# A shifted copy of V sent in three parts, and new order lists for all five engines

## The chip, the core and the metric

The kernel runs on one core of one Trainium2 chip. That core has five instruction streams that matter here: TensorE (PE, matrix multiplication, with PEld for its weight loads), VectorE (DVE), ScalarE (ACT), GpSimd (POOL) and SyncE (SP), which in this kernel only issues DMAs. SBUF is the on-chip memory of 128 partitions, and PSUM is the memory of eight banks that PE writes into. The metric is the device time in microseconds (us) of one execution. Most executions of one kernel agree within 0.3%.

## The reference

The kernel computes a fused mixer on 2048 tokens of width 512, in bf16: a sliding, dilated local attention, a gated MLP that mixes over tokens, and the residual.

```python
def _A_ref(x, wqkv, wo):                     # 32 heads of 16, window 8, dilation 2
    qkv = (x @ wqkv).reshape(B, S, 3, H, Dh).transpose(2, 0, 3, 1, 4)
    q, k, v = qkv[0], qkv[1], qkv[2]
    idx = pos[:, None] - off[None, :]        # off = 0, 2, ..., 14
    mask = idx >= 0
    ...
    logits = jnp.einsum('bhsd,bhswd->bhsw', q, kg) * scale
    logits = jnp.where(mask[None, None, :, :], logits, -1000000000.0)
    attn = _softmax(logits, axis=-1)
    o = jnp.einsum('bhsw,bhswd->bhsd', attn, vg)
    return o.transpose(0, 2, 1, 3).reshape(B, S, D) @ wo

def _B_ref(x, w_in, w_sp, b_sp, w_out):      # Fh = 896
    z = _gelu(jnp.einsum('bsd,df->bsf', x, w_in))
    z1 = z[..., :Fh].copy()
    z2 = _layernorm(z[..., Fh:], axis=-1)
    g = jnp.einsum('ts,bsf->btf', w_sp, z2) + b_sp[None, :, None]
    return jnp.einsum('bsf,fd->bsd', z1 * g, w_out)

x = A_x
xn = _layernorm(x, axis=-1)
return x + _A_ref(xn, A_wqkv, A_wo) + _B_ref(xn, B_w_in, B_w_sp, B_b_sp, B_w_out)
```

## The kernel before, in words

**Layout.** The 2048 tokens are cut into 16 blocks of 128. In the working layout a token is 16 times its partition plus its block number q, so that one block holds every sixteenth token. The keys of a token lie 0, 2, ..., 14 tokens back. A token of block q therefore needs the values V of blocks q, q-2, ... on its own partition, and where q-2i is negative, it needs block q-2i+16 of the partition before it. For these the kernel keeps a shifted copy: 14 columns of tokens in front of V, in which partition p+1 holds what partition p holds in blocks 2 to 15. It is made by two DMAs from SBUF to SBUF, Vhaloa for partitions 0 to 111 and Vhalob for 112 to 126 (L1155), and by Vzero (L1158), which puts zeros on partition 0. The products of the probabilities with V (pv0 to pv15, L1178, one DVE instruction for each block) read both V and the copy; pv14 and pv15 need no copy, since they reach back 14 tokens at most.

**Order.** The program is a list of about 760 tasks. `Plan` (L15 to L285) derives the waits from what each task reads and writes (keys with address ranges; ranges that overlap depend on each other), and gives each engine a queue of its own with one semaphore. The order in each queue isn't found by a planner here: `plan.orders` (from L1277) holds five written lists, for PE, ACT, DVE, POOL and SP, and names every task of the engine in turn. An engine works strictly down its list. A task that isn't ready holds up all that stand behind it.

**Stages on PE**, with names as the lists have them (block or group number behind the name):

- Start: the first block is centred on DVE and ACT (ctr), transposed on PE (xTr, L691), evacuated from PSUM by ACT (xTe, L698), and multiplied into z2 for blocks 0 to 3 in half pieces (z2_b_h, L900). xNr (L711) transposes the normalized first block (norm0, L675). Blocks 4 to 15 are transposed by DMA on SP's queue (xTd, L679).
- Q and K (L743, evacuated by ACT, QKe at L751) in four groups of blocks, with the rest of z2 (L877, evacuated as z2g) between them. z2s (L932) are ACT's squares of z2 for the layer norm; zm0, zq, zv, zr, zb are its small sums, of which zr (L949) runs on POOL and zb (L951) on DVE. hm (L583) are masks made on POOL.
- Logits: DVE multiplies Q with shifted K (prod, L766) and adds pairs (padd, L774); PE sums them (lg, L801); ACT evacuates them (lge, L810). Then z1 (L920, z1g) and V (L727, evacuated by ACT as Ve, L731).
- Softmax on DVE (sm, ssub, sz, L826 to L867), whose probabilities are transposed in by DMA (pT, L819).
- The token mixing: for each of eight groups t, PE does seven products P1 to P7 of 8 matmuls each (L1038), with the spatial weights w (loaded transposed by DMA, w1_0 and so on, L985), and their sums S13, S2, S4, made on DVE (L997 to L1003). The gating follows (g11, g21 on ACT, L1056; g12, g22 on DVE, L1080 and L1084; u, L1062; uT, a DMA transposition, L1064).
- pv, pva, pvc on DVE (L1178 to L1186) make the attention's output, OTd (L1190) transposes it by DMA, and out (L1240, L1244) multiplies both halves by their output weights. os and fin copy the result out of PSUM with the residual, and st (L1215) stores it.

SP's queue holds, in this order around the copy of V: pT3, pT2, pT0, pT1, w1_0, w1_1, Vhalob, Vhaloa, w2_0, w2_1, uT14. The dependency of the copy is all of V from block 2 on, and by its ranges, which name one element in each of two buffers for the logits' products, all the work on these too.

Of the kernel before, what the change touches and what calls it, by code (L numbers as in the profile page):

```python
# [14 lines left out]
class Plan:  # L15
# [301 lines left out]
    warm=28,  # L317
    fill0=1,
# [9 lines left out]
def build_kernel(nc, A_x, A_wqkv, A_wo, B_x, B_w_in, B_w_sp, B_b_sp, B_w_out, out, report=False, sched_kw=None,  # L328
# [5 lines left out]
    NB = S // 128  # L334
# [17 lines left out]
    off = {}  # L352
# [66 lines left out]
    with ExitStack() as es:  # L419
        ar = es.enter_context(nc.sbuf_tensor("arena", [128, ARENA_E], BF))  # L420
# [27 lines left out]
        R = plan.reg  # L448
# [38 lines left out]
        for i, nm in enumerate("abz"):  # L487
            R("Vh" + nm, "sb", [(off["pb"] + 4096 * s_ + 1024 + i, off["pb"] + 4096 * s_ + 1025 + i) for s_ in range(2)])
# [61 lines left out]
        def dma(eng, fn, nbytes, chan, reads=(), writes=(), name="", xbar=False, prio=None, lat=1700.0):  # L550
# [12 lines left out]
          name="steps0")  # L563
# [590 lines left out]
        for nm, p0, p1 in (("a", 0, 112), ("b", 112, 127)):  # L1154
            dma("sp", (lambda p0, p1: lambda e: e.dma_start(  # L1155
                ar[p0 + 1: p1 + 1, off["V"] - 14 * 512: off["V"]], ar[p0: p1, off["V"] + 1024: off["V"] + 8192]))(p0, p1),
                (p1 - p0) * 14 * 1024, "Vh" + nm, reads=[("V", q) for q in range(2, NB)], writes=["Vh" + nm], name="Vhalo" + nm)
# [102 lines left out]
        for t in range(NT):  # L1260
# [11 lines left out]
            if t >= 1:  # L1272
# [6 lines left out]
                warm xTr0b fill0 xTr0a z2_0_0b z2_0_1b z2_0_0a xTr1a xTr1b z2_0_1a xNr z2_1_0a z2_1_0b z2_1_1a xTr2a  # L1279
                xTr2b z2_1_1b z2_2_0a z2_2_0b xTr3b xTr3a z2_2_1a z2_2_1b z2_3_0a z2_3_1a z2_3_1b z2_3_0b Q0_0 Q0_2  # L1280
                Q0_1 K0_1 Q0_3 K0_0 K0_2 K0_3 Q1_0 K1_0 K1_1 Q1_1 Q1_2 K1_2 K1_3 Q1_3 z2_4 z2_5 z2_6 z2_7 K2_0 K2_1
                Q2_1 Q2_0 K2_2 Q2_2 z2_8 Q2_3 K2_3 z2_9 z2_10 z2_11 K3_0 Q3_1 K3_1 K3_2 Q3_2 Q3_0 z2_12 z2_13 K3_3
                Q3_3 lg0_0 z1_14 z2_15 z2_14 z1_13 z1_12 z1_15 z1_11 z1_8 z1_10 z1_6 z1_9 z1_7 z1_5 z1_4 z1_2 z1_0
# [12 lines left out]
                lge1 zn6 z1g12 z1g13 z1g15 z2s13 z1g11 z2s14 z1g8 z1g10 zn4 halo2_0 halo2_1 z1g6 z2s15 z1g9 z1g7 zn7
                z1g5 zn11 z1g4 z1g2 zn8 z1g0 zn0 z1g3 zn3 Ve12 Ve13 z1g1 Ve15 Ve14 lge2 ldxr0 lge3 Ve9 Ve10 zn9 Ve7
                Ve11 Ve6 ldxr1 Ve8 zn10 Ve4 Ve5 sexp3 Ve2 cA_0 Ve1 Ve3 Ve0 cE_0 cB_0 g11_0 os12_0 os15_0 sexp2 cA_1
                cE_1 g21_0 cB_1 g11_1 cA_2 sexp1 g11_2 os14_0 cB_2 cE_2 fin15_0 g21_1 g21_2 cA_3 cB_3 ldxr2 fin14_0
                g11_3 cE_3 os13_0 fin12_0 sexp0 cA_4 st0_0_0 g21_3 cB_4 fin13_0 g11_4 os11_0 os10_0 cE_4 ldxr3 cA_5  # L1300
                fin11_0 os8_0 ldxr4 st1_0_0 cB_5 fin10_0 cE_5 os9_0 g11_5 g21_4 os6_0 ldxr5 cA_6 cE_6 g21_5 cB_6 g11_6
                st2_0_0 fin8_0 os7_0 fin9_0 ldxr6 fin6_0 cA_7 os4_0 fin7_0 os2_0 os5_0 st3_0_0 cB_7 ldxr7 cE_7 g21_6
                g11_7 st4_0_0 fin5_0 os0_0 fin4_0 st5_0_0 g21_7 os3_0 fin2_0 fin3_0 os1_0 st6_0_0 os1_1 fin0_0 os1_2
# [15 lines left out]
                g22_5 pvc4 g12_5 u7 S2_6 pv4 pv5 u5 u4 pva2048_5 S4_6 pva1024_5 S13_7 sattn0 pvc5 g22_6 pv3 g12_6 pv2
# [65 lines left out]
```

## Time and profile before

| | us |
|---|---|
| runs | 226.03, 226.43, 226.57 (median 226.43) |
| the profiled execution | 226.05 |
| its span | 224.3 |
| PE busy | 220.5 (98%) |
| DVE busy | 207.6 (93%) |
| ACT busy | 134.2 (60%) |
| POOL busy | 92.8 (41%) |
| DMA engines, mean share by q1 and q10 | 56.6% and 6.6% |

The span runs from the first to the last instruction of the core; the execution's own time lies 1.75 us above it. In the rows of the profile a number behind L is the line of the kernel. "A <- B" means that A waited for B, "xN" is the number of instructions in a group, and an engine name with q behind it (SPq) is that engine's DMA queue. The chain of waits lists, in order of time, the pieces of work that set the end, each with its start, its length and its line. In the table by stage each engine has its busy time in the window and, in brackets, its instructions. "Us to landing" is the time from a DMA's issue to the arrival of its data.

### The profile page before, as it was taken

The page shows a single profiled execution, that of the slowest core. Times are in us where ns is not written, and L with a number is a line of the kernel's source. Part 1 is how long each engine was busy: PE and PEld are TensorE (multiplying, and loading weights), DVE is VectorE, ACT ScalarE, POOL GpSimd, SP SyncE. Part 2 cuts the span into 40 slices and gives each one's busy share as a digit, 9 for nine tenths or more (in the row PEclk, how much of TensorE's full clock was granted, in tenths as well). Part 3 has the DMA queues.
Part 4 walks back from the last instruction along what each step waited for, and adds up shares of the span by engine and source line. Part 5 has one row for each costly group of instructions (what it writes and reads, how often), then busy time and mean ns, then how long its engine had stood idle before and what let it go on. Part 6 is the DMA issues. An engine that isn't in the chain of part 4 may idle for free.

```text
span 224.3 us, 3127 instructions
## 1 busy us (share of the span) xinstructions
PE 220.5 (98%) x1176; PEld 121.4 (54%) x1176; DVE 207.6 (93%) x236; ACT 134.2 (60%) x241; POOL 92.8 (41%) x38
## 2 busy tenths in 40 slices
PE   7999999999999999999999999999999999999995
PEld 6555555554577775665555544445545544455444
DVE  4699999899999999999999999999999999999910
ACT  4758989989999999987332321525115433242442
POOL 4348289826054071000000399992899920000000
PEclk9999999999999999999999999999999999999999
DMA  6886443491000005759899896495996792729442
GB/s 218 261 200 155 63 115 69 78 274 26 3 0 0 0 0 167 172 122 220 223 154 197 215 223 120 122 217 107 139 213 167 156 173 71 163 85 168 102 92 94
DMA packets 77400, 29.96 MB, mean 134 GB/s; under 512 B 68669, under 2 KB 75339, under 8 KB 77259
## 3 DMA queue, kind: packets, MB, share of 16 engines
q1 hardware_dynamic: 74250, 25.08, 56.6%
q10 hardware_dynamic: 3136, 4.69, 6.6%
q8 instruction: 9, 0.15, 0.3%
q14 instruction: 5, 0.04, 0.0%
HBM read 9.05 MB, written 2.10 MB: 50 GB/s over the span
## 4 chain that ended last, share of the span: by engine, by line
PE 90%; DVE 4%; issue 2%; ACT 2%; DMA 1%; ACTq 0%
PE ps L1038 38%; PE ps L920 11%; PE ps L1244 11%; PE ps L743 9%; PE ps L727 6%; PE ps L1240 6%; PE ps L877 5%; DVE arena L774 3%; PE ps L900 3%; DMA arena<-in_A_x_dram 1%; PE ps L801 1%; ACT arena L751 0%; PE ps L691 0%; ACT arena L932 0%; ACT arena L883 0%
## 5 line engine op out<-in xcount | busy, mean ns | idle before, releaser
L1038 PE MATMUL ps<-arena 128*128 128x448 f16 (+1 forms) x448 | 86.6, 352 | 0.0
L860 POOL TENSOR_TENSOR arena<-arena,fpool 128x128 bf16<-128x128 f32 x2 | 48.5, 24274 | 47.1 <-DVE arena L856 47.1
L1038 PEld LDWEIGHTS ps<-arena 128*128 128x128 f16 (+1 forms) x448 | 43.7, 98 | 41.4 <-issue 0.2
L1178 DVE TENSOR_TENSOR arena<-arena 128x4096 bf16<-128x4096 bf16 x16 | 36.1, 2282 | 0.0
L766 DVE TENSOR_TENSOR arena<-arena 128x8192 bf16<-128x8192 bf16 (+1 forms) x10 | 35.5, 3558 | 0.0
L949 POOL TENSOR_TENSOR fpool<-fpool 128x4 f32<-128x4 f32 x4 | 21.0, 5255 | 25.4 <-DVE fpool L946 25.4
L743 PE MATMUL ps<-arena 128*128 128x512 bf16 x128 | 28.5, 379 | 0.0
L1182 DVE TENSOR_TENSOR arena<-arena 128x4096 bf16<-128x4096 bf16 (+1 forms) x16 | 28.0, 1749 | 0.0
L1253 ACT ACTIVATE arena<-ps 128x512 bf16<-128x512 f32 (+2 forms) x17 | 9.6, 563 | 30.6 <-PE ps L1244 30.6
L1244 PE MATMUL ps<-arena 128*128 128x512 bf16 (+2 forms) x126 | 27.1, 355 | 0.0
L774 DVE TENSOR_TENSOR arena<-arena 128x4096 bf16<-128x4096 bf16 (+1 forms) x9 | 27.0, 2995 | 0.0
L665 POOL TENSOR_TENSOR fpool<-fpool 128x1 f32<-128x1 f32 x16 | 18.8, 1183 | 14.5 <-DVE fpool L663 14.5
L1053 ACT ACTIVATE ps<-ps 128x448 f32<-128x448 f32 x16 | 8.5, 528 | 27.2 <-PE ps L1038 19.2
L920 PE MATMUL ps<-arena 128*128 128x448 bf16 x128 | 24.6, 353 | 0.0
L920 PEld LDWEIGHTS ps<-arena 128*128 128x128 bf16 x128 | 18.4, 144 | 6.1 <-issue 0.4
L743 PEld LDWEIGHTS ps<-arena 128*128 128x128 bf16 x128 | 14.4, 113 | 13.1 <-issue 0.4
L877 PE MATMUL ps<-arena 128*128 128x448 bf16 x96 | 19.0, 353 | 0.0
L1244 PEld LDWEIGHTS ps<-arena 128*128 128x128 bf16 x126 | 11.9, 98 | 12.4
L751 ACT ACTIVATE arena<-ps 128x1024 bf16<-128x1024 f32 x16 | 16.0, 1028 | 4.2 <-PE ps L743 3.5
L1240 PE MATMUL ps<-arena 128*128 128x512 bf16 (+2 forms) x72 | 16.8, 355 | 0.0
L932 ACT ACTIVATE arena<-arena 128x896 bf16<-128x896 bf16 x16 | 15.4, 965 | 0.0
L1056 ACT ACTIVATE arena<-ps,fpool 128x448 bf16<-128x448 f32 x16 | 10.0, 633 | 7.9 <-PE ps L1038 7.9
(86 smaller groups left out, 255.8 us busy)
## 6 DMA issues: line engine op xcount, KB each, us to landing
arena<-in_A_x_dram ACTq DMA_DIRECT2D x8, 256.0 KB, 2.8
arena<-in_A_x_dram SPq DMA_DIRECT2D x15, 128.0 KB, 2.3
out_dram<-arena ACTq DMA_DIRECT2D x7, 256.0 KB, 2.1
arena<-arena SPq DMA_DIRECT2D x1, 1568.0 KB, 11.1
arena<-in_A_wqkv_dram SPq DMA_DIRECT2D x3, 512.0 KB, 4.0
arena<-in_B_w_in_dram SPq DMA_DIRECT2D x1, 896.0 KB, 5.4
arena<-in_B_w_out_dram SPq DMA_DIRECT2D x1, 896.0 KB, 5.0
arena<-arena SPq DMA_TRANSPOSE x40, 3.2
```

The lines of the kernel that those rows point to most:

```text
L743: last = t.matmul(bank(k + which), AC(off["wqk"] + 1024 * dc + col0, [[4, 128]]), AC(off["xnT"] + dc * S + 512 * j, [[1, 512]]), start=(dc ...
L766: T("dve", lambda v: v.tensor_tensor(pbv, qb, kb, ALU.mult), reads=[(t_, c, j) for t_ in ("QT", "KT", "KTpad") for c in cs], writes=[("pb" ...
L774: T("dve", lambda v: v.tensor_tensor(av, av, bv, ALU.add), reads=[("pb", s_) for s_ in b], writes=[("pb", s_) for s_ in a], est=c_dve(4096 ...
L860: T("pool", lambda g: g.tensor_tensor(Rv, Zv, FCa(foff["mone"], [[0, 128]]), ALU.pow), reads=[kz, "mone"], writes=[kr], est=20000, name="s ...
L877: last = t.matmul(ps[:, 512 * (k + hf): 512 * (k + hf) + HF], AC(off["xnT"] + dc * S + 128 * b, [[1, 128]]), AC(off["w_in2"] + FH * dc + H ...
L920: lastm = t.matmul(ps[:, 512 * (k + hf): 512 * (k + hf) + HF], AC(off["xnT"] + dc * S + b, [[NTOK, 128]]), AC(off["w_in1"] + FH * dc + HF ...
L949: T("pool", lambda g: g.tensor_tensor(Fv("rstd2", 4, 4 * j), Fv("msq", 4, 4 * j), mhalf, ALU.pow), reads=[("msq", j), "mhalf"], writes=[(" ...
L1038: last = t_.matmul(pb_(k_), st(k), mv(k), start=(start and k == 0), stop=(k == 7), skip_group_check=True)
L1178: T("dve", (lambda iv, tv, av: lambda v: v.tensor_tensor(tv, iv, av, ALU.mult))(iv, tv, av), reads=[("attn", q // 4)] + [("V", i_) for i_ ...
L1182: T("dve", (lambda n: lambda v: v.tensor_tensor(AC(off["Vs"], [[4096, 2], [1, n]]), AC(off["Vs"], [[4096, 2], [1, n]]), AC(off["Vs"] + n, ...
L1240: t_.matmul(po, AC(off["OT"] + 1024 * (t % 3) + 512 * r_ + 128 * cc, [[1, 128]]), AC(off["wo"] + 512 * cc + c0, [[1, n]]), start=False, st ...
L1244: last = t_.matmul(po, AC(off["z1"] + FH * tb + 128 * fc, [[1, 128]]), AC(off["w_out"] + 512 * fc + c0, [[1, n]]), start=False, stop=(fc = ...
```

## The change

The shifted copy gets three groups of token columns instead of one: the four columns just before V (blocks 12 to 15), the four before them (blocks 8 to 11) and the last six (blocks 2 to 7). Each group is sent in the same two parts by partitions as before, so there are six DMAs (Vhalo0a to Vhalo2b) instead of two. Each waits only for its own blocks of V. Its address range names one element at its own destination. A product pv needs only the groups that it reaches into: pv10 to pv13 group 0, pv6 to pv9 groups 0 and 1, pv0 to pv5 all three.

All five order lists are written anew. Besides the six DMAs they hold the same tasks. No instruction of PE, ACT, DVE or POOL is added, removed or resized. In the kernel after, lines from the copy on stand 4 to 13 further down.

```diff
-        for i, nm in enumerate("abz"):
-            R("Vh" + nm, "sb", [(off["pb"] + 4096 * s_ + 1024 + i, ...) for s_ in range(2)])
+        VH = ((1, 4), (5, 8), (9, 14))
+        vh = lambda g_, i: off["V"] - 512 * VH[g_][1] + i
+        for g_ in range(3):
+            for i in range(2):
+                R(("Vh", g_, i), "sb", [(vh(g_, i), vh(g_, i) + 1)])
+        R("Vhz", "sb", [(vh(g_, 2), vh(g_, 2) + 1) for g_ in range(3)])
...
-        for nm, p0, p1 in (("a", 0, 112), ("b", 112, 127)):
-            dma("sp", (lambda p0, p1: lambda e: e.dma_start(
-                ar[p0 + 1: p1 + 1, off["V"] - 14 * 512: off["V"]], ar[p0: p1, off["V"] + 1024: off["V"] + 8192]))(p0, p1),
-                (p1 - p0) * 14 * 1024, "Vh" + nm, reads=[("V", q) for q in range(2, NB)], writes=["Vh" + nm], name="Vhalo" + nm)
+        def v_halo(g_):
+            lo, hi = VH[g_]
+            o_, n = off["V"] - 512 * hi, 512 * (hi - lo + 1)
+            for i, (p0, p1) in enumerate(((0, 112), (112, 127))):
+                dma("sp", (lambda p0, p1: lambda e: e.dma_start(ar[p0 + 1: p1 + 1, o_: o_ + n], ar[p0: p1, o_ + 8192: o_ + 8192 + n]))(p0, p1),
+                    (p1 - p0) * 2 * n, ("Vh", g_, i), reads=[("V", q) for q in range(16 - hi, 17 - lo)], writes=[("Vh", g_, i)],
+                    name="Vhalo%d%s" % (g_, "ab"[i]))
+        for g_ in range(3):
+            v_halo(g_)
...
-                  reads=[...] + (["Vha", "Vhb", "Vhz"] if q < 14 else []),
+                  reads=[...] + (["Vhz"] if q < 14 else []) + [("Vh", g_, i_) for g_ in range(3) for i_ in range(2) if q < 15 - VH[g_][0]],
...
 plan.orders, PE:
-  warm xTr0b fill0 xTr0a z2_0_0b z2_0_1b z2_0_0a xTr1a xTr1b z2_0_1a xNr z2_1_0a z2_1_0b z2_1_1a xTr2a
+  warm xTr0b fill0 xTr0a xNr z2_0_0b z2_0_1b xTr1a z2_0_1a xTr1b z2_0_0a z2_1_0a z2_1_1a xTr2a z2_1_0b
...
-  P1_1 P4_0 P5_1 bits P6_1 P2_1 P7_1 P3_1 P1_2 P4_1 P2_2 P5_2 P6_2 P1_3 P7_2 P3_2 out15_0 P4_2 out14_0
+  P1_1 P4_0 P5_1 P6_1 P2_1 P7_1 P3_1 P1_2 P4_1 P5_2 P6_2 P2_2 P7_2 P3_2 P1_3 P4_2 P5_3 P2_3 P6_3 out15_0
...
 ACT:
-  zn2 QKe3_1 z2s10 QKe3_2 QKe3_0 zn1 z2g12 z2g13 halo2_3 z2s11 QKe3_3 lge0 zn5 z1g14 z2s12 z2g15 z2g14
+  QKe3_2 halo2_0 halo2_3 zn3 QKe3_0 z2g12 zn1 z2g13 QKe3_3 lge0 halo2_2 z2s10 z1g14 z2s11 z2g15 z2g14
...
 DVE:
-  prod1_2 zq1 zb0 prod1_0 zv1 padd1_0 padd1_1 zb1 zq2 prod2_0 prod2_2 zv2 padd2_0 prod3_2 zq3 padd2_1
+  prod1_0 zb0 prod1_2 zq1 padd1_0 zq2 padd1_1 zv1 prod2_0 prod2_2 zq3 zb1 padd2_0 zv2 prod3_2 zv3
...
-  srec3 sm2_2 sattn3 sm3_2 pv15 pv14 g22_0 ssub2 S13_1 g12_0 sz1_2 S2_1 u14 sz2_2 pva2048_0 S4_1
+  sm1_2 srec3 sm2_2 sattn3 sm3_2 pv15 pv14 g22_0 ssub2 g12_0 S13_1 sz1_2 S2_1 sz2_2 pva2048_0 sm1_1 u15
...
 POOL:
-  rstd5 rstd10 rstd11 rstd9 mask1 rstd8 rstd14 rstd13 rstd12 rstd15 hm2 zr0 zr1 zr2 zr3 srec1 srec0
+  rstd5 rstd10 rstd8 rstd9 mask1 rstd11 rstd14 rstd15 rstd13 rstd12 zr0 hm2 zr1 zr2 zr3 srec1 srec0
...
 SP:
-  ldx0 ldx1 ldw_in2a_0 ldw_in2b_0 ldx3 ldx6 ldx7 ldx4 ldq ldx5 ldx9 ldx10 ldk ldx11 xTd6 xTd7 xTd4 xTd5
+  ldx0 ldx1 ldw_in2a_0 ldw_in2b_0 ldx3 ldx7 ldx6 ldx4 ldq ldx5 ldx10 ldk ldx9 ldx8 xTd7 xTd6 xTd4 xTd5
...
-  ldwout Vzero pT3 pT2 pT0 pT1 w1_0 w1_1 Vhalob Vhaloa w2_0 w2_1 uT14 w3_0 uT15 OTd0 ldwo0 ldwo3 ldwo2
-  ldwo1 w3_1 w4_0 uT12 OTd1 uT13 w4_1 w5_0 uT11 uT10 OTd2 w5_1 w6_0 uT8 w6_1 uT6 uT9 w7_0 OTd3 uT7 w7_1
+  ldwout pT3 pT2 Vhalo0a Vhalo1b pT0 w1_0 w1_1 pT1 w2_0 ldwo3 ldwo2 Vzero w2_1 ldwo0 Vhalo2b ldwo1
+  Vhalo0b uT14 w3_0 uT15 w3_1 uT12 OTd0 w4_0 uT13 w4_1 Vhalo1a uT11 OTd1 w5_0 uT10 w5_1 OTd2 Vhalo2a uT8
```

More of the change, by code (lines that the diff above doesn't have):

```diff
@@ L1278, in build_kernel @@
             """
-                warm xTr0b fill0 xTr0a z2_0_0b z2_0_1b z2_0_0a xTr1a xTr1b z2_0_1a xNr z2_1_0a z2_1_0b z2_1_1a xTr2a
[L1280 to L1283, printed above, removed]
@@ new lines, in build_kernel @@
+                xTr2b z2_1_1b z2_2_1a xTr3a xTr3b z2_2_0a z2_2_1b z2_2_0b z2_3_1a z2_3_0a z2_3_1b z2_3_0b Q0_0 Q0_2
+                Q0_1 K0_1 Q0_3 K0_0 K0_2 K0_3 K1_0 Q1_0 Q1_1 K1_1 K1_2 Q1_2 Q1_3 K1_3 z2_4 z2_5 z2_6 z2_7 Q2_0 K2_0
+                K2_1 Q2_1 Q2_2 Q2_3 K2_3 z2_8 K2_2 z2_10 z2_11 z2_9 K3_1 Q3_1 K3_2 Q3_2 Q3_0 K3_0 z2_12 z2_13 Q3_3
+                K3_3 lg0_0 z1_14 z2_15 z2_14 z1_13 z1_12 z1_15 z1_8 z1_11 z1_10 z1_7 z1_6 z1_9 z1_2 z1_5 z1_4 z1_1
+                z1_0 z1_3 V13 V12 V10 V14 lg2_0 V11 V15 V4 V7 V6 V8 V9 V5 V1 V0 V3 V2 P1_0 P5_0 P6_0 P2_0 bits P7_0
@@ L1297, in build_kernel @@
[L1297 to L1301, printed above, removed]
@@ new lines, in build_kernel @@
+                z2s5 QKe2_0 z2s6 QKe2_1 z2s7 halo1_0 QKe2_3 z2g8 QKe2_2 z2s8 z2g10 zn2 z2g11 halo1_3 z2g9 QKe3_1 z2s9
+                QKe3_2 halo2_0 halo2_3 zn3 QKe3_0 z2g12 zn1 z2g13 QKe3_3 lge0 halo2_2 z2s10 z1g14 z2s11 z2g15 z2g14
+                z2s12 z1g13 z2s13 z1g12 z1g15 zn5 z1g8 z2s14 z1g11 z2s15 z1g10 z1g7 halo2_1 zn6 z1g6 z1g9 zn0 z1g2
+                lge1 z1g5 z1g4 zn11 z1g1 z1g0 zn7 z1g3 Ve13 Ve12 zn4 Ve10 zn10 lge2 lge3 Ve15 Ve14 zn8 Ve11 Ve7 Ve6
+                zn9 Ve9 Ve8 ldxr0 Ve4 Ve5 sexp3 Ve2 Ve1 cA_0 Ve3 Ve0 cB_0 g11_0 os14_0 cE_0 sexp2 cA_1 os15_0 g21_0
@@ L1317, in build_kernel @@
-                u11 S4_3 pva2048_2 g22_3 S13_4 sm3_0 g12_3 ssub0 S2_4 pva1024_2 sz1_0 S4_4 pvc2 u8 sz2_0 pv9 pv8 sz3_0
-                pva2048_3 g22_4 pva1024_3 g12_4 S13_5 u9 u6 sattn1 pvc3 S2_5 pv7 pv6 S4_5 pva2048_4 S13_6 pva1024_4
-                g22_5 pvc4 g12_5 u7 S2_6 pv4 pv5 u5 u4 pva2048_5 S4_6 pva1024_5 S13_7 sattn0 pvc5 g22_6 pv3 g12_6 pv2
-                S2_7 pva2048_6 S4_7 pva1024_6 u2 pvc6 pv1 u3 pv0 g12_7 g22_7 u0 pva2048_7 pva1024_7 pvc7 u1 fin1_1
+                zeros steps0 steps1 bnst0 bnag0 ctr1 bnst1 bnag1 norm0 norm1 bnst2 bnag2 bnst3 norm2 bnag3 norm3 bnst7
```

51 lines of the change are left out of this document (27 added, 24 removed).

## The prediction

> **What bounds the kernel now.** I read the page's first part, then a table by stage, then the waits of TensorE (PE) and VectorE (DVE), then the chain.
>
> ```profile
> span 224.3 us, 3127 instructions
> PE 220.5 (98%) x1176; PEld 121.4 (54%) x1176; DVE 207.6 (93%) x236; ACT 134.2 (60%) x241; POOL 92.8 (41%) x38
> ```
>
> PE is busy for 98% of the span and DVE for 93%. The stages from the first real matmul to the last one show how little is idle:
>
> ```profile
> core 0: us, PE busy (x) PEld busy (x) DVE busy (x) ACT busy (x) POOL busy (x), PEclk, DMA share, GB/s
> 4.40:12.70 8.30, 8.11 (x55) 4.13 (x56) 6.20 (x16) 6.65 (x23) 3.07 (x8) 1.00 0.93 293
> 12.70:55.60 42.90, 42.80 (x208) 22.01 (x206) 41.73 (x51) 37.99 (x76) 29.27 (x16) 1.00 0.53 116
> 55.60:99.20 43.60, 43.54 (x241) 29.94 (x242) 43.50 (x39) 42.70 (x61) 10.35 (x2) 1.00 0.23 58
> 99.20:222.10 122.90, 122.82 (x648) 62.29 (x645) 114.55 (x128) 44.82 (x83) 48.55 (x2) 1.00 0.80 156
> ```
>
> Of 217.70 us PE is idle for 0.19 + 0.10 + 0.06 + 0.08 = 0.43, at a granted clock of 1.00 throughout. No order of the same matmuls can win much more than that and the pipeline refills behind each wait. Of the waits that are on record, two bear on the change most:
>
> ```profile
> PE ps L801 <- DVE fpool L943: 0.2, 1, 0.2
> ...
> DVE fpool L660 <- DMA arena<-in_A_x_dram: 1.7, 1, 1.7
> ```
>
> The second row is the only wait of DVE for a DMA in the whole run: the products of V (L1178) never waited for the shifted copy. The copy thus costs nothing today, and splitting it saves nothing directly.
>
> **The change against the chain.** The chain of waits gives PE's pace (448 columns: 6.05/32 = 0.189 us each) and the places where it falls behind it.
>
> ```profile
> 12.64 13.91 PE ps L743 x64
> 26.55 6.05 PE ps L877 x32
> 32.61 5.18 PE ps L743 x24
> ...
> 55.67 1.04 PE ps L801 x16
> ...
> 58.38 3.18 PE ps L877 x16
> ...
> 112.85 18.16 PE ps L1038 x96
> ```
>
> *Start of PE's list.* xNr, the transposition of the normalized first block, moves ahead of the first z2 matmuls.
>
> ```profile
> 4.72 0.27 PE L691 MATMUL ps<-arena 128*128 128x128 bf16 x2
> 5.11 0.37 DVE L675 TENSOR_SCALAR arena<-arena,fpool 128x512 bf16<-128x512 bf16 x1
> 5.17 1.41 PE L900 MATMUL ps<-arena 128*128 128x448 bf16 x6 [0.18 <-ACT arena L698]
> ```
>
> Its input, norm0, ends at 5.11 + 0.37 = 5.48, so PE now waits from 4.72 + 0.27 = 4.99 to about 5.50 instead of 5.17. In it stand 32 matmuls of 448 columns (32 x 0.189 = 6.05), twelve transpositions of blocks 1 to 3 and xNr's four, of 128 columns each (16 x 0.189 x 128/448 = 0.86): 6.91. With 0.16 to refill the pipeline (the pair of the row at 4.72 took 0.27, against 2 x 0.054 at pace) the stage ends at 5.50 + 0.16 + 6.91 = 12.57. Before it ends at 12.64, though 5.17 + 6.91 is 12.08: 0.5 went into small waits for transposed inputs, which the new list spreads out (xNr and three more transpositions stand ahead, so ACT has longer for the copies). I take -0.07; bounds +0.33 (the later start, and nothing won back) and -0.2.
>
> *xTd5.* 64 matmuls of 512 columns at the pace of the row with 24 (5.18/24 = 0.216) are 13.81; the row shows 13.91. The 0.10 is Q1_0 behind the last DMA transposition of blocks 4 to 7. The order of these four changes (7, 6, 4, 5 for 6, 7, 4, 5) while block 5 stays last. I take half: -0.05, bounds 0 and -0.10; a landing that comes later than before would cost its lateness, at most some 0.5.
>
> *zb0 and the first logits.* In the old POOL list hm2 stands before zr0, and DVE's zb0 waits for zr0:
>
> ```profile
> 36.17 2.55 POOL L583 TENSOR_SCALAR_AFFINE_SELECT arena<-arena 128x32 bf16<-128x32 bf16 x1
> ```
>
> ```profile
> 44.22 0.16 DVE L951 SCALAR_TENSOR_TENSOR fpool<-fpool 128x4 f32<-128x4 f32 x1 [0.84 <-POOL fpool L949]
> ```
>
> The new list has zr0 first, about 2.5 us sooner, and its zb0 stands behind a product. The 0.84 goes, and with it every product behind it comes that much sooner, padd1_1 (L774) too, for which PE waits 0.2 at lg0_0 (L801, 55.67): -0.20, bounds 0 and -0.22. Next late would be ScalarE (ACT) with the banks that lg0_0 overwrites.
>
> *z2_15.* 16 matmuls at 0.189 are 3.03, the row shows 3.18: z2_15 waits 0.15 for lge0 to free its banks.
>
> ```profile
> 55.42 0.97 ACT L932 ACTIVATE arena<-arena 128x896 bf16<-128x896 bf16 x1
> 57.25 1.05 ACT L810 ACTIVATE arena<-ps 128x1024 bf16<-128x1024 f32 x1
> ```
>
> In the new ACT list z2s11 (55.42) goes behind lge0 (57.25), which then follows QKe3_3 up to 0.9 sooner: -0.15, bounds 0 and -0.15. What surrounds these places keeps its number of instructions on each engine; only SP gets four more.
>
> *The copy itself.* Two issues of 210 and 1568 KB become six: 448 and 60 KB twice, 672 and 90 KB once; bytes are the same.
>
> ```profile
> 90.73 7.37 SPq L819 DMA_TRANSPOSE arena<-arena  x4
> 99.23 4.21 SPq L985 DMA_TRANSPOSE arena<-in_B_w_sp_dram  x2
> 103.49 1.50 SPq L1155 DMA_DIRECT2D arena<-arena  x2
> 105.28 13.00 SPq L985 DMA_TRANSPOSE arena<-in_B_w_sp_dram  x2
> L985 SPq DMA_TRANSPOSE arena<-in_B_w_sp_dram x16: 2032/2336/9887, 42.1 to 180.1; - x16
> DMA to landing us min/median/max: 4.2/4.8/13.3
> arena<-arena SPq DMA_DIRECT2D x1, 1568.0 KB, 11.1
> ...
> arena<-arena SPq DMA_DIRECT2D x1, 210.0 KB, 5.7
> ...
> out_dram<-arena SPq DMA_DIRECT2D x2, 48.0 KB, 1.5
> ```
>
> An issue costs SP 0.75; four more are 3.0 us of a queue that mostly waits. What counts is the line behind them: w2_0, issued right after the copy, held SP for 9.89 us instead of 2.34, until the copy was down, and landed 13.3 after 105.28, at 118.6. P1_2, which needs it, is the fifth group of the chain row at 112.85: 112.85 + 32 x 0.189 = 118.90. It had 0.3 to spare. Now the blocking is cut up. Vhalo0a and Vhalo1b stand before pT0 and the w1 loads; parts 2b and 0b before uT14; 1a before uT11; 2a before uT8. By size a 448 KB part lands after 11.1 x 448/1568 = 3.2 at the least, and after 5.7 at the price of the 210 KB one; a 60 KB part between 1.5 and 5.7. I take 3 for each, the size-proportional value, and keep 5.7. What is nearest is w1, the second load of the row at 99.23: issued at 99.23 + 2.10 = 101.3, and landed at 106.1 with the median 4.8. S13_1, its first user, starts here:
>
> ```profile
> 95.93 1.32 ACT L731 ACTIVATE arena<-ps 128x512 bf16<-128x512 f32 x2
> ```
>
> ```profile
> 109.42 1.22 DVE L997 TENSOR_TENSOR arena<-arena 128x2048 f16<-128x2048 bf16 x1
> 110.56 0.68 DVE L1080 SCALAR_TENSOR_TENSOR arena<-ps,fpool 128x448 bf16<-128x448 f32 x1
> ```
>
> Vhalo1b waits for Ve8, which stands one place earlier among the copies of V than Ve4 did, the first of the two at 95.93: done by 95.93 + 0.66 = 96.6. At 3.0 the part lands at 99.6; pT0 then takes 1.84 (7.37/4), and the w1 loads start at 101.4, 2.2 later than at 99.23. w1_1 lands at 108.3, still before S13_1 at 109.42. I take 0. pv13, the first product that needs a part, comes at about 124; 0a, 0b and the zero row are issued by 116 and land by 122 even at 5.7. pv9 and pv5 have more room. w2_0 is issued at about 105 with no copy in front and lands near 110, 9 us before P1_2.
>
> The Trainium skill, page "DMA: Bandwidth & Descriptors", section "Bandwidth", speaks against such a split: DMAs should be batched to 1 MiB or more, and those under 64 KB are dominated by their descriptors; its section on the anatomy of a DMA puts the fixed part at about 2 us. An estimate by that page is four more fixed parts, 8 us of queue. The trace bears out that small copies are dear (210 KB in 5.7 us) but shows them landing under other work.
>
> *DVE's tail of the softmax.* g12_0 (L1080, 0.60 a turn) now stands before S13_1, which P5_1 needs. Before, S13_1 ended at 110.64 and P5_1 began on the chain at 112.85 - 8 x 0.189 - 0.03 (bits, one tiny matmul) = 111.31: 0.67 to spare. After: 0.67 - 0.60 + 0.84 (DVE's lead) - 0.47 (PE's own gain) = 0.44. No cost; without DVE's lead 0.40 would be lost.
>
> The sum: -0.07 - 0.05 - 0.20 - 0.15 = -0.47 on the profiled execution, which took 226.05 (span 224.3, 1.75 around it) and lies 0.38 below the median of 226.43. I set it against the median: 226.0. The tail (last matmul, its copy, its store) is the same in both lists.
>
> **The rivals.** *Faster by more than 0.3%.* P1_2 had 0.3 us to spare against a DMA that was blocked for 10. If the other two runs lost their extra time there, the change takes that too: 226.43 - 0.38 - 0.47 = 225.6. For it: the nearness. Against it: nothing in the profiled run shows such a wait, and the start of a run varies as well.
>
> *Slower: a transposition blocked behind a part.* The 9.89 us shows that a transposition holds SP until a copy in front has landed. pT0 stands behind Vhalo0a and Vhalo1b as w2_0 did behind the whole copy, and the w1 loads stand behind pT0. It decides from the point where a part lands 1.1 us later than the 3.0 taken (109.42 - 108.3), plus 0.44 of slack at P5_1, so from 4.5 us on. At 5.7 the w1 loads are 2.7 us later still, w1_1 lands at 111.0, and P5_1 waits 1.1: 227.1. If the 448 KB part takes the whole copy's 11.1, from about 93.3 (pT3 and pT2 at 1.3 to 1.8 each after 90.73) to 104.4, w1 starts at 106.2, w1_1 lands at 113.1 and P5_1 waits 3.2: 229.2. Midway is 228.1. For it speaks that the 210 KB copy took half as long as one seven times its size, against it that the 210 KB one shared its time with two loads and the large copy. The page named above adds no price of its own here: of its four fixed parts one stands ahead of w1.
>
> *The change does nothing:* the PE waits move instead of going (norm0 late, ACT behind at lg0_0): +0.33 with nothing won, 226.4 to 226.8.
>
> **How the numbers follow.** About 0.3%, 0.68 us, is what a measurement here can tell from no change, so "same" runs from 225.75 to 227.11. The forecast (0.36) and the empty change (0.16) make 0.52 for within 0.3%; the faster rival has 0.26, its bound being only 0.25 from the forecast; the blocked transposition, midway, has 0.16 and waits in the new lists that no row foretells 0.06, together 0.22. The range: below, the 0.47, the 0.38 and another 0.23 of small waits gone, 225.35; above, between the blocked transposition's two prices, 227.6; the forecast's own is 225.75 to 226.6.
>
> **What would show it.** Right: PE's wait at L801 and DVE's at L951 gone, the wait at L900 replaced by one of 0.4 to 0.5 at L711 behind L675, no wait of DVE for a DMA after 5 us, the longest transposition of L985 far below 9.9 us. Wrong: PE waiting at L1042 (the old L1038) for L997's sums or for a landing; DVE waiting at the products for a part of the copy; a stage after 55 us in which PE idles by more than 0.2.

## The result and the profile after

The changed kernel takes 225.83 us (median of 15 runs, 225.54 to 226.54), the kernel before 226.43 us (15 runs, 226.03 to 226.97). The ratio is 0.997, with a 95% interval of 0.9957 to 0.9983: faster by 0.3%, 0.4 to 1.0 us. In a second set of runs on another occasion it was 225.83 again, against 226.53 (ratio 0.9974, 0.9956 to 0.9993). Three executions of 475 to 604 us, two of the kernel before and one of an experiment, were disturbed and are left out throughout.

The two profiled executions don't show this gain: 226.07 us after and 226.05 before, with a span of 224.3 us in both. One has to look by stage. Lines of the changed kernel stand 4 further down up to the copy and 7 to 9 from there on (L691 is L695, L1038 is L1042). This is the page's first part for it:

```profile
span 224.3 us, 3131 instructions
PE 220.9 (98%) x1176; PEld 122.7 (55%) x1176; DVE 207.5 (92%) x236; ACT 135.3 (60%) x241; POOL 90.5 (40%) x38
```

The same four stages, again with the busy time of each engine:

```profile
core 0: us, PE busy (x) PEld busy (x) DVE busy (x) ACT busy (x) POOL busy (x), PEclk, DMA share, GB/s
4.40:12.70 8.30, 8.00 (x53) 4.60 (x51) 6.51 (x18) 5.18 (x16) 3.57 (x7) 1.00 0.95 297
12.70:55.60 42.90, 42.90 (x211) 22.34 (x208) 41.63 (x47) 39.79 (x80) 23.13 (x16) 1.00 0.61 115
55.60:99.20 43.60, 43.60 (x243) 29.99 (x242) 43.53 (x41) 42.73 (x63) 11.94 (x3) 1.00 0.21 54
99.20:222.10 122.90, 122.83 (x648) 62.31 (x645) 113.99 (x126) 45.33 (x83) 49.95 (x2) 1.00 0.74 157
```

PE's idle time is now 0.00 in the second and third stage, 0.07 in the last, and 0.30 in the first. The waits of PE on record, and the one of DVE for a DMA:

```profile
PE ps L636 <- PEq L1379: 0.8, 1, 0.8
PE ps L715 <- DVE arena L679: 0.3, 1, 0.3
...
DVE fpool L664 <- DMA arena<-in_A_x_dram: 1.5, 1, 1.5
```

The wait at the first logits and the wait at the first z2 have gone. A wait of 0.3 at xNr (now L715) is new. The chain of waits shows what each stage is worth:

```profile
5.36 0.61 PE ps L715 x4
5.96 1.21 PE ps L904 x4
...
13.14 13.81 PE ps L747 x64
...
55.90 0.98 PE ps L805 x16
...
58.55 3.03 PE ps L881 x16
61.57 22.70 PE ps L924 x120
```

The 64 matmuls of Q and K take 13.81 (13.91 before), the logits 0.98 (1.04), z2_15 and z2_14 3.03 (3.18): all at pace. But Q begins at 13.14 where it began at 12.64. PE thus won 0.50 behind the start and lost 0.50 in the start. The row at 5.96 says how: four matmuls of 448 columns took 1.21, or 0.30 each, and not 0.189. A matmul at a slower pace counts as busy all the while, so neither the table by stage nor the idle time shows this loss.

What became of the copy is in the list of SP's DMAs, the rows for the loads of w, and the landings:

```profile
93.68 3.73 SPq L1162 DMA_DIRECT2D arena<-arena  x2
97.45 1.31 SPq L823 DMA_TRANSPOSE arena<-arena  x1
99.24 4.79 SPq L989 DMA_TRANSPOSE arena<-in_B_w_sp_dram  x2
...
105.50 2.57 SPq L989 DMA_TRANSPOSE arena<-in_B_w_sp_dram  x1
L989 SPq DMA_TRANSPOSE arena<-in_B_w_sp_dram x16: 2013/2258/5172, 28.3 to 180.3; - x16
arena<-arena SPq DMA_DIRECT2D x2, 448.0 KB, 4.6
arena<-arena SPq DMA_DIRECT2D x1, 672.0 KB, 5.2
...
arena<-arena SPq DMA_DIRECT2D x2, 60.0 KB, 2.8
```

pT0, behind the first two parts, leaves SP in 1.31 us; the w1 loads go at 99.24 as before; w2_0 takes 2.57 us of SP instead of 9.89, and landed at 110.1, 8.7 us ahead of P1_2.

### The profile page after: what moved, and what is told of

It reads as the page before. It is cut to its first block, busy times and chain, and to the rows that moved or that the text cites. A ratio compares the mean times of both kernels' runs of the same rounds, so it can differ in the third digit from the quotient of the medians.

```text
span 224.3 us, 3131 instructions
## 1 busy us (share of the span) xinstructions
PE 220.9 (98%) x1176; PEld 122.7 (55%) x1176; DVE 207.5 (92%) x236; ACT 135.3 (60%) x241; POOL 90.5 (40%) x38
## 4 chain that ended last, share of the span: by engine, by line
PE 97%; DVE 1%; DMA 1%; ACT 0%; issue 0%
PE ps L1042 38%; PE ps L747 12%; PE ps L924 11%; PE ps L1253 11%; PE ps L881 8%; PE ps L731 6%; PE ps L1249 6%; PE ps L904 3%; DMA arena<-in_A_x_dram 1%; PE ps L805 1%; DVE fpool L664 1%; PE ps L695 0%; PE ps L715 0%; DVE fpool L667 0%; DVE arena L679 0%; DVE arena L672 0%
## 5 line engine op out<-in xcount | busy, mean ns | idle before, releaser
L1042 PE MATMUL ps<-arena 128*128 128x448 f16 (+1 forms) x448 | 86.4, 352 | 0.0
L864 POOL TENSOR_TENSOR arena<-arena,fpool 128x128 bf16<-128x128 f32 x2 | 50.0, 24978 | 53.0 <-DVE arena L860 53.0
L1042 PEld LDWEIGHTS ps<-arena 128*128 128x128 f16 (+1 forms) x448 | 43.8, 98 | 41.3
L953 POOL TENSOR_TENSOR fpool<-fpool 128x4 f32<-128x4 f32 x4 | 15.6, 3906 | 19.4 <-DVE fpool L950 19.4
```

What stands on the lines that cost most here:

```text
L864: T("pool", lambda g: g.tensor_tensor(Rv, Zv, FCa(foff["mone"], [[0, 128]]), ALU.pow), reads=[kz, "mone"], writes=[kr], est=20000, name="s ...
L1042: last = t_.matmul(pb_(k_), st(k), mv(k), start=(start and k == 0), stop=(k == 7), skip_group_check=True)
```

## The experiments

Below, "Q0_0 to out" is the time from the end of PE's first task of Q to the end of its last matmul, and the stages are cut at the ends of lg0_0, z2_15 and V2. All are read from the moments at which PE reported the tasks as done; they leave the start out, so two traces can be compared to some hundredths. "Pace doubles at" is the time at which PE's matmuls go over from one of 448 columns every 0.37 us to one every 0.189; the last section has more on it.

| trace | pace doubles at | Q0_0 ends | to lg0_0 | to z2_15 | to V2 | to out | w2_0 lands |
|---|---|---|---|---|---|---|---|
| before | 3.5 | 13.52 | 43.21 | 3.33 | 39.16 | 122.82 | 118.58 |
| before_b | 5.5 | 13.72 | 43.13 | 3.33 | 39.16 | 123.93 | 119.83 |
| before_c | 3.5, half again 6.9 to 10.3 | 16.18 | 43.13 | 3.33 | 39.16 | 123.80 | 121.96 |
| split_only | 4.0 | 13.62 | 43.15 | 3.41 | 39.15 | 122.82 | 109.67 |
| split_two_waits | 6.6 | 14.24 | 42.89 | 3.16 | 39.50 | 122.82 | 110.16 |
| waits_only | 6.3 | 14.04 | 44.40 | 3.16 | 39.50 | 125.04 | 122.49 |
| orders_only | 9.9 | 15.91 | 42.89 | 3.16 | 39.16 | 125.50 | 122.10 |
| orders_pt1_first | 5.1 to 5.9 | 13.87 | 42.89 | 3.16 | 39.15 | 125.58 | 118.66 |
| w2_ahead_again | 4.1 to 4.7 | 13.99 | 43.12 | 3.33 | 39.16 | 123.08 | 109.84 |
| after | 6.6 | 14.02 | 42.89 | 3.17 | 39.16 | 122.82 | 110.08 |
| after_again | 4.7 to 5.3 | 13.97 | 42.89 | 3.16 | 39.16 | 122.82 | 109.76 |
| after_oldstart | 3.9 | 13.64 | 42.91 | 3.16 | 39.16 | 122.82 | 109.84 |

### The changed kernel once more

No edit.

> The changed kernel once more, as it stands. From the first Q matmul (L747) to the last matmul PE took 222.04 - 13.14 = 208.90 us in its profile, against 222.03 - 12.64 = 209.39 before: 0.49 won there. The first stage lost the same 0.50 (Q began at 13.14, not 12.64). Theory A: that loss belongs to the PE clock, whose matmuls of 448 columns came every 0.38 us until about 6.8 us in this profile but every 0.189 from 3.5 us on in the profile before; then 208.90 comes again within 0.05, while the begin of Q moves between about 12.5 and 13.2 with the moment at which the matmuls double their pace. Theory B: it belongs to xNr's new place (a wait of 0.3 for norm0); then Q begins at 13.1 again whatever the pace. The time is 225.8 +- 0.3 in both.

It took 225.83 (225.73 to 227.56, 11 runs). From the first Q matmul to the end it is 222.00 - 13.10 = 208.90 again; Q0_0 to out is 208.03 in this trace, 208.02 in the first, and 208.52 before: 0.49 won, with 0.32 up to the first logits (the waits at Q1_0 and lg0_0) and 0.17 at z2_15. Not all of this is the change's. The 0.10 at Q1_0 stands in the first trace of before alone. In the other traces of the table with the old order of the DMA transpositions (xTd6, xTd7, xTd4, xTd5) the second group of Q and K follows the first without a wait, as this row of before_b shows (64 matmuls at pace):

```profile
12.84 13.81 PE ps L743 x64
```

From the end of Q0_0 to that of V2 the traces of before take 85.61 to 85.70, those of the changed kernel 85.21: the change wins 0.4 to 0.5 there. The begin of Q is the open point. Here PE's pace had doubled by 5.34, earlier than in the first trace, and yet Q0_0 ends at 13.97. These rows of PE's timeline (start, length, instructions, and in brackets the idle time before) show why:

```profile
5.34 0.40 PE L715 MATMUL ps<-arena 128*128 128x128 bf16 x4 [0.33 <-DVE arena L679]
5.58 0.92 PE L904 MATMUL ps<-arena 128*128 128x448 bf16 x4
...
7.08 0.54 PE L904 MATMUL ps<-arena 128*128 128x448 bf16 x2 [0.47 <-ACT arena L702]
```

PE waits 0.33 for norm0, and then 0.47 in front of z2_0_1a. The profile names ACT for that; the last load of w_in2 (in2b_0) landed at 6.95, and z2_0_1a, which multiplies with it, began at 7.08. The old list has z2_0_0a and xTr1b ahead of z2_0_1a as well, and neither needs this load. So theory A, the pace alone, doesn't explain this trace, and of theory B the wait for norm0 is there. But the larger wait is for a load that came late: it landed at 6.42 in the first trace of the changed kernel and at 6.50 in orders_pt1_first, which has the same start and no such wait. And with the old start and this load at 7.00, w2_ahead_again ends Q0_0 at 13.99.

### The new lists with the old copy

```diff
 copy: as before (two parts, one dependency on V from block 2 on)
 SP:
-  ldwout pT3 pT2 Vhalo0a Vhalo1b pT0 w1_0 w1_1 pT1 w2_0 ldwo3 ldwo2 Vzero w2_1 ...
+  ldwout Vzero pT3 pT2 pT0 w1_0 w1_1 pT1 Vhalob Vhaloa w2_0 ldwo3 ldwo2 w2_1 ...
```

> The new order lists with the copy in its two old parts, which stand ahead of w2_0 as before. Theory A (the gain is the PE waits that the lists take away, the copy costs nothing): 0.997 of before as for the whole change, 208.9 us from the first Q matmul to the last matmul, though w2_0 is held for 9 to 10 us again. Rival C (the runs of before lost time to w2_0, which landed 0.3 us ahead of P1_2): most of the gain is gone, 0.9985 or more, and PE waits at L1038 for a landing near 119 us in some traces.

It took 231.39 us (229.28 to 231.87, 6 runs), 1.0206 of before (1.0169 to 1.0242). From V2 to out it lost 2.7 us: w2_0 landed at 122.10 and P1_2 waited for it, then P5_2. The lists' own gain is there (42.89 and 3.16) and is spent at w2_0. Theory A was wrong that the copy costs nothing. In part the new SP order is to blame: pT1 stands behind the w1 loads, so that the copy goes out 5.8 us after V2 and not 4.3. The median lies 4.9 above that of before, though. In the traced run (230.62) some 2 us come from the start, where the pace doubled only at 9.9; whether this is so in the other five isn't known.

### The new lists with the old copy, and pT1 first

```diff
-  ldwout Vzero pT3 pT2 pT0 w1_0 w1_1 pT1 Vhalob Vhaloa w2_0 ...
+  ldwout Vzero pT3 pT2 pT0 pT1 w1_0 w1_1 Vhalob Vhaloa w2_0 ...
```

> The new lists with the old copy, as before, but pT1 ahead of w1_0 again, so that the copy goes out 1.3 us sooner than with the new lists' SP order. In the first run of the new lists with the old copy w2_0 landed at 122.10 and P1_2, P5_2 waited: from the end of V2 to PE's end 125.49 us where it is 122.81 before. If the lists need the split only for that (theory F), w2_0 now lands 19.4 after the end of V2 as before, P1_2 begins on time or up to 0.5 late, and the time is 225.9 to 226.6. If anything else in the lists needs it, it stays above 228.

It took 229.29 us (228.06 to 230.81, 4 runs), ratio 1.0125 (1.0065 to 1.0185). Now w2_0 lands at 118.66, which costs P1_2 only 0.2, and still 2.8 us are lost. Rows of the waits of PE and DVE:

```profile
PE ps L1038 <- DVE arena L997: 1.9, 1, 1.9
...
DVE arena L997 <- DMA arena<-in_B_w_sp_dram: 3.2, 1, 3.2
```

S13_2 waits 3.2 us for w2_1, which lands at 122.52 behind the copy, and P5_2 waits for S13_2. The new DVE list has S13_2 some 2.5 us earlier (begin 119.46 in the changed kernel, 121.93 before), and the new PE list has P5_2 one product earlier, ahead of P2_2. Theory F falls: in the changed kernel these weights land at 110.08 and 115.81, and without the split the new lists are slower than the old ones.

### The split copy with the old lists

```diff
 copy: in three groups, as in the changed kernel
 SP:
-  pT3 pT2 pT0 pT1 w1_0 w1_1 Vhalob Vhaloa w2_0 w2_1 uT14 ...
+  pT3 pT2 Vhalo0a Vhalo1b pT0 pT1 w1_0 w1_1 w2_0 w2_1 Vhalo2b Vhalo0b uT14 ... Vhalo1a uT11 ... Vhalo2a uT8
```

> The old order lists with the copy in six parts: 0a and 1b ahead of pT0, 2b and 0b ahead of uT14, 1a ahead of uT11, 2a ahead of uT8. Theory A: no change, 1.000 +- 0.001; 209.4 us from the first Q matmul to the last matmul, w2_0 lands near 110 us and not at 118.6, P1_2 is not sooner for it. Rival C: 0.997 to 0.9985. Rival D (a transposition is held behind a part): w1_0 issued late, S13_1 after 109.42, up to 228.

It took 226.25 us (226.05 to 226.84, 12 runs), ratio 0.9987 (0.9974 to 0.9999). Q0_0 to out is 208.53, as in the first trace of before (208.52), and the lowest time is the same (226.05, 226.03). What is gone are the long runs: of the 25 runs of before beside it 6 lie above 227.0, of these 12 none. So the split is worth nothing in a good run. That it is worth something in others is what the medians say, and it has a cause in the next traces; the count of long runs alone is too small to show it.

### Two more traces of the kernel before

No edit.

> The kernel before once more, for its trace: its runs spread over 226.0 to 227.7, those of the split copy only over 226.05 to 226.84. Rival C: in a long run w2_0 lands after P1_2 could begin and PE waits at L1038 near 119 us. Theory A: the spread is the start alone, in which PE's first matmuls come at half the pace until somewhere between 3.5 and 6.8 us; then PE takes 208.5 us from the end of Q0_0 to its own end in this trace too (222.03 - 13.52 = 208.51 in the first).

> As the run ahead of it: a third trace of the kernel before, for how w2_0's landing and the start vary. Rival C asks for a PE wait near 119 us in a long run, theory A for 208.5 us from the end of Q0_0 to PE's end.

They took 227.30 and 229.62 us. Rows of before_b: SP's DMA, the wait, and PE's matmuls.

```profile
105.87 13.64 SPq L985 DMA_TRANSPOSE arena<-in_B_w_sp_dram  x2
PE ps L1038 <- DMA arena<-in_B_w_sp_dram: 0.9, 1, 0.9
119.96 6.21 PE L1038 MATMUL ps<-arena 128*128 128x448 bf16 x32 [0.95 <-DMA arena<-in_B_w_sp_dram]
```

w2_0 landed at 119.83 in this run, and by PE's pace P1_2 could have begun at 118.85. It began at 119.96, and from V2 to out the run lost 1.11. before_c has the same wait (0.6) and lost 0.78 by it, and another 0.20 at out15_0. The first trace of before, with w2_0 landing 0.16 us ahead of P1_2, was the only one of the three without a wait. Even this margin is smaller than it looks: where P1_2 had to wait, it began 0.13 to 0.14 after the landing (119.83 and 119.96 here, 121.96 and 122.10 in before_c). Rival C holds. The rest of before_c's length is its start. Its first load of x landed at 4.26 (3.09 in the first trace), PE stood idle for it, and though the pace had already doubled at 3.5, it fell back to half from 6.9 to 10.3. In this trace the granted clock shows it (the wait, then windows of PE: busy, instructions, clock, DMA share, GB/s):

```profile
PE ps L691 <- DVE arena L668: 1.5, 1, 1.5
...
core 0: us, PE busy (x), PEclk, DMA share, GB/s
...
4.20:7.00 2.80, 1.23 (x9) 0.98 1.06 350
7.00:10.00 3.00, 3.00 (x15) 0.50 0.85 249
10.00:13.00 3.00, 3.00 (x21) 0.95 1.03 334
```

### w2_0 ahead of the old copy

```diff
-  w1_0 w1_1 Vhalob Vhaloa w2_0 w2_1 uT14
+  w1_0 w1_1 w2_0 Vhalob Vhaloa w2_1 uT14
```

> The kernel before with one change: w2_0 stands ahead of the two parts of the copy on SP instead of behind. Rival C (the longer ones among the runs of before are those in which w2_0 lands after P1_2 could begin): they go, as with the split copy; the lowest time stays at 226.05, the median falls by 0.2 to 0.4. If the clock's opening alone makes the spread, the spread stays as before and the median falls by less than 0.1. w2_0 lands near 108, w2_1 is now the one that is held, until 116, and lands near 120.5, which S13_2 at 121.9 can bear.

> The kernel before with w2_0 ahead of the copy, once more, for a trace of an undisturbed run. The copy now holds w2_1. Its 11 undisturbed runs were no shorter than those of before (226.36 to 227.87). Rival C in a second form: w2_1 lands at 121 to 122, beside P2_2 (121.8) and S13_2 (121.9), so the hazard has only moved by one load; theory A: w2_1 lands well ahead of both and PE has no wait there.

The 11 runs of w2_ahead_of_copy have a median of 226.89 us (ratio 1.001, 0.9993 to 1.0027). The trace is that of w2_ahead_again, a single run of 226.69:

```profile
107.82 1.51 SPq L1155 DMA_DIRECT2D arena<-arena  x2
111.73 8.18 SPq L985 DMA_TRANSPOSE arena<-in_B_w_sp_dram  x1
```

w2_0 lands at 109.84, but now w2_1 is held for 8.18 us and lands at 121.93. That is 0.4 ahead of S13_2 (begin 122.33), and neither DVE nor PE waits there: P2_2 and P5_2 end as long after V2 as in the first trace of before. From V2 to out it is 123.08, 0.26 more than in a good run, and all of it stands in front of out15_0. The last weights that this task needs (ldwo1, further down in SP's queue) landed at 131.37, and it began at 131.50. So the hold does hand a wait on, but to another load than the second form of rival C says. Of the 11 runs 4 lie above 227.0, which this one trace doesn't explain.

### The whole copy ahead of the w1 loads

```diff
-  pT0 pT1 w1_0 w1_1 Vhalob Vhaloa w2_0
+  pT0 pT1 Vhalob Vhaloa w1_0 w1_1 w2_0
```

> The kernel before with the whole copy, in its two parts, ahead of w1_0. It goes out when Ve0 is done, about 103.3, and lands near 114.5. If a transposition is held until the copy has landed (rival D), w1_0 leaves SP at 114.3, w1_1 lands near 119, S13_1 and P5_1 are 9 to 10 us late, and the time is 235 to 236. If only the issue of four descriptors counts, w1_1 lands near 109 and the time stays at 226 to 227.

It took 236.66 us (two runs), ratio 1.0447. The copy went out at 102.41 and landed at 114.05:

```profile
103.95 19.94 SPq L985 DMA_TRANSPOSE arena<-in_B_w_sp_dram  x4
PE ps L1038 <- DMA arena<-in_B_w_sp_dram: 7.8, 1, 7.8
...
DVE arena L997 <- DMA arena<-in_B_w_sp_dram: 10.2, 1, 10.2
```

w1_0 held SP from 103.95 until w1_1 followed at 113.76, 0.3 us before the copy was down, as w2_0 did in the kernel before. This is the blocked transposition of the prediction at full size, and its price is 10 us. Not all of it is waiting. PE's first matmul of P1_1 begins at 116.23, 8.0 after its turn, and from there until 121.0 a matmul of 448 columns comes every 0.373 us; the mean granted clock of the run is 0.978. P1_1 ends 9.5 late and P4_0 10.3: the wait costs another 2.3 in pace.

### Three waits, and two, alone

waits_only, on the kernel before, and split_two_waits, on the split copy with the old lists (that one without the third line):

```diff
 POOL:  - hm2 zr0      + zr0 hm2
 ACT:   - z2s11 QKe3_3 lge0      + QKe3_3 lge0 z2s11
 SP:    - xTd6 xTd7 xTd4 xTd5      + xTd7 xTd6 xTd4 xTd5
```

> The kernel before with three changes in its order lists: hm2 behind zr0 on POOL, z2s11 behind lge0 on ACT, xTd7 ahead of xTd6 on SP. Theory A: PE's waits at lg0_0 (0.20), z2_15 (0.15) and Q1_0 (0.05 to 0.10) go and 0.40 is won: 209.0 us from the first Q matmul to the last matmul, 0.998 of before. Rival E (each wait is replaced by another): 209.3 to 209.4, 1.000.

> The old lists with the split copy, and two moves: hm2 behind zr0 on POOL, z2s11 behind lge0 on ACT. Theory A: PE's waits at lg0_0 (0.2) and at z2_15 (0.15) go, from Q0_0's begin to PE's end 209.2 us where the split copy alone has 209.58; the time is 225.9, 0.35 below that of the split copy alone. Rival E (other waits take their place): 209.5, 226.25.

waits_only took 227.96 us (ratio 1.0076, 1.0049 to 1.0103), slower than before. The third line was ill chosen, as the second of these waits of PE shows:

```profile
PE ps L1038 <- DMA arena<-in_B_w_sp_dram: 1.8, 1, 1.8
PE ps L743 <- DMA arena<-arena: 1.3, 1, 1.3
```

xTd7 needs norm7, which the old DVE list makes after norm6; ahead of xTd6 it holds both up, until 13.50 instead of 11.53. The change under study turned the normalizations round as well. The later SP and DVE then made w2_0 late for P1_2 (the first row). split_two_waits, free of both, took 226.22 us (ratio 0.9985, 0.9971 to 0.9999), the same as the split alone. Its trace has the full gain up to z2_15 (42.89 and 3.16), and then 39.50 instead of 39.16 up to V2. The chain of waits runs over ACT there:

```profile
61.87 1.80 ACT arena L887 x4
63.66 0.92 ACT arena L814
64.58 1.02 ACT arena L960
65.60 0.82 ACT arena L930
...
66.46 18.38 PE ps L924 x96
```

ACT is busy for 42.2 of the 43.6 us of this stage. A wait of 0.35 of PE at z1_11 is new: rival E, in part. z2s11, put off behind lge0, is the likely cause. The changed kernel keeps the gain (39.16). Its ACT list puts zn5, zn6 and lge1 off as well, and its PE list has z1_8 ahead of z1_11; which of the two does it wasn't tried.

### The changed kernel with the old start

```diff
 PE:
-  warm xTr0b fill0 xTr0a xNr z2_0_0b z2_0_1b xTr1a z2_0_1a xTr1b z2_0_0a ...
+  warm xTr0b fill0 xTr0a z2_0_0b z2_0_1b z2_0_0a xTr1a xTr1b z2_0_1a xNr ...
 ACT: as before up to the first evacuation of Q
```

> The changed kernel with the start of PE's and ACT's lists as before (up to the first Q matmul and the first evacuation of Q): z2_0_0b and z2_0_1b ahead of xNr, xTr1a and xTr1b ahead of z2_0_1a. Theory B2 (the new start costs 0.35 us when the clock opens early: 0.3 waiting for norm0, 0.5 for the last load of w_in, which the old start covers): Q0_0 begins at 12.5 to 12.6 with an early opening, not 12.93; from there to the end 209.06 as in the changed kernel; the time is 0.1 to 0.3 below that of the changed kernel, about 225.6. Theory A2 (the start costs nothing): the same as the changed kernel within 0.1.

It took 225.72 us (225.47 to 226.61, 10 runs), ratio 0.9967 (0.9951 to 0.9982), the lowest median of all. Q0_0 ends at 13.64 and not at 13.97, as theory B2 has it, though 225.72 and 225.83 are too close to be told apart, and the load in2b_0 landed at 6.52 here and at 6.95 there. The starts have to be set against each other like for like. With an early doubling and this load at 6.4 to 6.6 the old start ends between 13.52 and 13.72, the new one at 13.87 (one trace). With the load near 7.0 they end at 13.99 (old, w2_ahead_again) and 13.97 (new, after_again). With a doubling at 6.3 to 6.6 it is 14.04 and 14.24 (old) against 14.02 (new). So the 0.3 that theory B2 gives to norm0 rests on one trace, and its 0.5 for the load isn't shown.

## Why the prediction was right, and where it wasn't

**The sum.** It was -0.47, to be set against a median: 226.0. Measured is 225.83, a fall of 0.60 with an interval of 0.4 to 1.0. The time lay in the range, 0.08 above the border between "same" and "faster", to which the prediction gave 0.52 and 0.26. That the size came out so near is in part luck: two of the four terms of the sum (the start and xTd5) weren't found as forecast, and what the copy costs was left out.

**zb0 and the logits, xTd5, z2_15.** -0.20 was named for the first logits and -0.15 for z2_15; 0.22 and 0.17 were found, each in the row that was named. The -0.05 of xTd5 was read from a wait that only the first trace of before has, so its order can't be shown to have won it. The prediction took the terms one by one, as if ACT could bear the moved squares. split_two_waits shows that it can't by itself: 0.34 came back at z1_11. In the changed kernel it doesn't come back, by the rest of the new lists.

**The start of PE's list.** -0.07 was the mis-sized term. With an early doubling of the pace and the load in2b_0 in time the new start costs 0.15 to 0.35 by one trace, about the upper bound of 0.33; in the other cases it costs nothing or wins up to 0.2. The wait for norm0 was right, and about in size (0.30 and 0.33, where 0.4 to 0.5 were named). What the step left out is the pace: it reckoned every matmul at 0.189, and the moment of the doubling, which differs from run to run, moves the end of the stage by more than the order of the list does.

**The copy.** "The copy thus costs nothing today" was the step that failed. It was read from DVE's waits and a single execution. In that one P1_2 began 0.16 us after w2_0 had landed (the prediction took 0.3, from the chain's rows); in both further traces PE waited 0.6 and 0.9 for it, and from V2 to the end 1.0 to 1.1 were lost. The -0.47 of the sum doesn't hold this term at all. The first rival named exactly this place and the nearness, and got 0.26. Its own estimate, 225.6, lies 0.2 below the measured median and 226.0 lies 0.2 above: both parts are at work, 0.4 to 0.5 that every traced run of the changed kernel has and about 1 us that some runs of before lose. How many do, three traces can't say.

**The blocked transposition.** The parts landed in 4.6 (448 KB) and 2.8 us (60 KB), where 3 was taken for both, and 4.5 was given as the point from which a blocked transposition decides. Still nothing was blocked. pT0 had to wait for Vhalo1b's issue until 97.4 anyway, when the large part was all but down (98.21), and w1_1 landed at 106.11, 3.2 us ahead of S13_1. But it wasn't that alone. In split_only pT0 went out at 96.08 and had left SP after 1.40 us, 1.25 ahead of the large part's landing at 98.73. uT8, right behind the 672 KB part, held SP for 2.96 instead of 1.3 and had left it 2.06 ahead of the landing. So the prediction's step that a transposition holds SP until the copy in front has landed fails for the parts; it is real for the whole copy, as copy_ahead_of_w1 shows. At what size it begins, no run shows.

**Against the split.** By the Trainium skill, page "DMA: Bandwidth & Descriptors", section "Bandwidth", DMAs should be batched to 1 MiB or more, which speaks against the split. (That page of the Trainium skill gives the fixed part of 2 us, which the prediction takes from it, for DMAs issued by GpSimd; these are issued by SP, whose six issues took 4.5 us in all where the two had taken 1.5.) By these landings small parts are indeed dear: 448 KB in 4.6 us are 97 KB/us, 1568 KB in 11.1 us are 141. But the split kernel is not slower, since what the large copy costs is the queue behind it, not its own time.

## What to carry to other kernels

A large copy in front of a DMA transposition on the same queue (1568 KB here) takes that queue for as long as it flies, while behind parts of up to 672 KB it was free again before the landing; so look in the queue's rows for the one transposition that took several times the median, and at how much its first user has to spare. A margin of 0.2 us in one trace is not a margin: take two or three traces of the kernel before, above all when its runs spread more than the change is worth. And order lists are tuned to landings as a whole: moves that each remove a wait in one row were worth next to nothing (two waits alone) or did harm (the new lists without the split) until the rest was moved with them.

## What the runs showed of the hardware

PE's matmuls run at half pace at first, one of 448 columns every 0.37 to 0.38 us instead of 0.189, and the moment at which they double moves from 3.5 to 9.9 us between executions that begin alike. These are rows of PE's timeline in the new lists with the old copy, where it came at 9.9:

```profile
6.32 1.70 PE L900 MATMUL ps<-arena 128*128 128x448 bf16 x4
...
8.99 1.81 PE L900 MATMUL ps<-arena 128*128 128x448 bf16 x6
```

Between 3.5 and 6.6 the end of Q0_0 moves by 0.5 to 0.7 us with it (old start), and by some 2 us when it comes at 9.9. In most traces the column of the granted clock stays at 1.00 all the while, for a plain reason: the first record of the clock stands near the doubling itself (3.56 in the first trace of before, 5.70 in before_b, 6.75 in the changed kernel), and where no record is the column has 1.00. So the pace of the matmuls is the sign to go by. A doubled pace can also be lost again. In before_c PE stood idle for 1.5 us, and the records of the clock change at 3.49 (to 1.00), 6.91 (to 0.50) and 10.32 (to 1.00); in copy_ahead_of_w1 a wait of 8.0 us was followed by 4.8 us at half pace. The Trainium skill, page "TensorE: Matmul & The Clock Gate", Part 1, tells of this: the array's clock is halved until a free-running window of about 3.4 us was busy, so the moment varies with the window's phase. The traces fit it: the records of before_c are 3.41 us apart, and in eleven of the twelve traces of the table the first doubling comes somewhere between 3.5 and 6.6, about the span of one such window. In the trace with 9.9 PE had stood idle for 0.33 us ahead of 4.73 and for 0.39 ahead of 5.94. That these waits cost it a further window is a reading of the rows and wasn't tried; orders_pt1_first had waits of 0.27 and 0.47 at the same places, and its pace doubled before 5.9.
